# A spectral filter and two gated MLPs on one Trainium2 core: new moments for the hand-made order, with the filter's product and sum behind the subtraction for the lower part of u

## The chip, the cores and the metric

The kernel runs on 1 core of one Trainium2 chip. The metric is device time in microseconds (us), the median of repeated runs. The profile is of one further execution. Engines are named PE (TensorE; PEld is its weight load), DVE (VectorE), ACT (ScalarE), POOL (GpSimd) and SP (SyncE, which issues all DMAs here).

## The reference

Three stages follow each other; B = 8, S = 3072, D = 256.

```
X = rfft(x, axis=1);  y = irfft(X * (filt_r + 1j*filt_i), n=3072)      # per batch
h = y @ w_in;  e = exp(h - max(h));  solu = h * e / sum(e)             # d_ff 1024
ln = (solu - mean) / sqrt(var + 1e-6) * g_ln;  x2 = ln @ w_out
h2 = x2 @ w_in2;  out = (h2 * sigmoid(1.702 * h2)) @ w_out2            # d_ff 2048
```

Everything is float32.

## The kernel before

**Precision.** A product of float32 quality is made of three fp32r matmuls: each operand is split into a high part (an ACT copy to fp32r) and a low part (a subtraction on DVE or POOL), and high*high, low*high and high*low are summed in PSUM.

**Stages.** `Filter` does the FFT filter for one or two batches: 12 steps per batch (`load_x`, `split_x`, `step1`, `store_a`), then 32 groups, each of which goes through nine steps: load (`load2`: gt, bt), `split_m`, `split_a`, `forward`, `swap`, `weigh`, `split_y`, `inverse`, `store_z`. `forward` reads the product f out of PSUM once on ACT (xs, L482) and once on DVE (pr, L485). `swap` exchanges the halves of xs by two DMAs (xw). `weigh` is the product and the sum of the change's name: two DVE instructions, xw = xw*fi (L497) and pr = pr + xw (L498). `split_y` splits pr for the inverse transform.

`First` does the first MLP for a pair of 128-row tiles (a = 0, 1), with 96 pairs in all: `load`, `y`, `y_lo` (xl, L638), `hidden` (L647, four blocks `hidden a f`), `top` (row maximum, L653), `exp` (L659), `weigh` (L672), `square` (L683), `norm` (L692), `shuffle` and `gather` (a trip through DRAM, L699, L705), `turn` (32x32 transposes, L709), `u_hi` (L717), `u_lo` (L720), `project` (L730, four blocks `project c f`), `x2_add`, `x2_hi`, `x2_lo` (L751). A block of `project` needs u of both tiles, so the first one needs `u_lo` of tile 1.

`Second` does the second MLP in 16 steps d per block of two pairs: `hidden` (L799), `tanh` (L806), `gate` (L811), `split_hi` (L817), `split_lo` (gl, L823), `output` (L838); then `finish` and `store`.

**Order.** Every step of every stage gets a moment, a number on a common scale on which a pair takes 16. The steps are then called in the order of their moments, and that is the order of the instructions in each engine's queue; an engine waits at the first instruction that isn't ready. The tables at the top of the file hold the moments: `FIRST` counts from the pair's own zero (two entries: tile 0, tile 1), `SECOND` from the step's own moment, `FILTER` from a slot in the pair ("slots": the groups take the first two), `DENSE` the same for the filter of batches 1 and 2, which has four groups in a pair.

```
r, o, v = 16.0 * (n - 1), First(n), FIRST
at(r + v[step.__name__][a], step, a)
...
for _, _, fn, args in sorted(plan, key=lambda s: s[:2]):
    fn(*args)
```

**Which pairs hold what.** Batch 0 is filtered ahead. While the 12 pairs of batch 0 run, the groups of batches 1 and 2 run (four per pair, 512 columns). Then the filters of batches 3 and 4, and of 5 and 6, each take six pairs of steps with no groups and 16 pairs with two groups (512 columns, "wide" here); the filter of batch 7 takes 16 pairs with two groups of 256 columns ("narrow"). The last 16 pairs have no filter.

Buffers that matter: `ps_h` has one buffer for h, `ps_m` two (yt, f, x2), gt and bt three, mt four, xw, pr, fh and fl two.

Of the kernel before, what the change touches and what calls it, by code (L numbers as in the profile page):

```python
# [36 lines left out]


FIRST = {
    "load": -19.13,  # L40
    "y": -15.7,
    "y_lo": -15.4,
    "hidden": ((-13.6, -11.61), (-3.5, -3.47)),
    "top": (-10.5, -2.4),
    "exp": (-9.6, -1.76),
    "weigh": (-8.86, -1.19),
    "square": (-8.06, 0.3),
    "norm": (-6.58, 0.38),
    "shuffle": (-5.5, 1.2),
    "gather": (-4.79, 1.94),  # L50
    "turn": (-1.56, 6.89),
    "u_hi": (-0.97, 7.3),
    "u_lo": (-0.15, 8.0),
    "project": ((9.4, 10.02), (10.62, 11.52)),
    "x2_add": (10.18, 12.74),
    "x2_hi": 12.79,
    "x2_lo": 13.64,
}

SECOND = {  # L60
    "tanh": 0.7,
    "gate": 1.19,
    "split_hi": 2.47,
    "split_lo": 3.19,
    "output": 4.92,
    "finish": 5.0,
    "store": 6.61,
}


FILTER = {
    "slots": (-0.46, 3.41, 4.53, 14.68),
    "first": (-5.35, -2.02, 0.2, 0.29),
    "second": (-4.91, -1.89, -2.29, -0.1, 1.84, 6.42, 12.49, 15.05, 15.71),
}


DENSE = {
    "start": 15.65,
    "slots": (0.77, 4.65, 8.65, 12.36),  # L80
    "second": (-6.78, -2.67, -1.85, -0.07, 0.61, 5.46, 7.59, 10.89, 10.96),
}

STAGE = [i % 5 if i < 15 else i % 3 for i in range(24)]
# [889 lines left out]
```

## Time and profile before

| | us |
|---|---|
| median of 3 runs | 3728.55 |
| the runs | 3726.52 to 3730.84 |
| span of the profiled execution | 3725.1 |
| PE busy | 3619.2 (97%) |
| DVE busy | 2719.4 (73%) |
| ACT busy | 2054.9 (55%) |
| POOL busy | 809.6 (22%) |

The span runs from the first to the last instruction of one profiled execution, whose own time is this span and what lies around it; the median of the three runs is 3.4 us above the span. A matmul's end is modelled, so the distance from one matmul's start to the next says more than its duration. In the timeline a row holds the start, the time, the engine, the line, the operation, out<-in and a count; a bracket gives the idle time ahead and what ended it.

### The profile page before, as it was taken

The numbers are of one execution on the slowest core, as the hardware profiler recorded it, in microseconds if no ns is written. First come the engines' busy times: TensorE is split into PE (matmuls) and PEld (weight loads), VectorE is DVE, ScalarE is ACT, GpSimd is POOL, SyncE is SP. The second block draws the span as 40 slices with busy tenths as digits, with TensorE's granted clock in tenths as the row PEclk, the third lists the DMA queues.
The fourth block names the chain that finished last, engine by engine and source line by source line (L and its number), as shares of the span: only waits on it lengthen the run. The fifth ranks groups of instructions, "written<-read, shape, count | busy, mean of one in ns | idle before, by whom it ended". The sixth has DMA issues, their size and how long they took to land.

```text
span 3725.1 us, 50469 instructions
## 1 busy us (share of the span) xinstructions
PE 3619.2 (97%) x16768; PEld 2938.3 (79%) x16768; DVE 2719.4 (73%) x4065; ACT 2054.9 (55%) x3762; POOL 809.6 (22%) x1349
## 2 busy tenths in 40 slices
PE   6779999999999999999999999999999999999999
PEld 2367778888888888888888888888888888888887
DVE  7768887667777777667777777667777777766675
ACT  2346665555555555555565656555555555554453
POOL 1123332222222221222222222122122221111110
PEclk7789999999999999999999999999999999999999
DMA  8735554434344433343344433333433332222221
GB/s 256 227 124 149 149 152 125 130 117 117 112 116 115 122 112 108 125 131 108 111 120 117 122 110 117 106 116 104 115 105 102 109 108 77 84 76 77 80 77 32
DMA packets 385669, 433.71 MB, mean 116 GB/s; under 512 B 144128, under 2 KB 294784, under 8 KB 385408
## 3 DMA queue, kind: packets, MB, share of 16 engines
q1 hardware_dynamic: 385408, 430.49, 39.4%
q8 instruction: 132, 2.16, 0.2%
q14 instruction: 129, 1.06, 0.1%
HBM read 232.13 MB, written 176.16 MB: 110 GB/s over the span
## 4 chain that ended last, share of the span: by engine, by line
PE 81%; DVE 8%; DMA 4%; issue 3%; ACT 2%; SPq 1%; POOL 1%; DVEq 0%; POOLq 0%; ACTq 0%
PE h L799 23%; PE o L838 23%; PE x L730 15%; PE h L647 12%; PE f L395 5%; PE yt L629 2%; DVE e L672 1%; DVE u L720 1%; DVE th L811 1%; SPq L861 1%; DMA xin<-in_x 1%; DMA xw<-xs 1%; DVE ob L849 1%; DMA out<-ob 1%; ACT xs L482 1%
## 5 line engine op out<-in xcount | busy, mean ns | idle before, releaser
L838 PE MATMUL o<-gh,w 128*128 128x512 f32 (+1 forms) x3136 | 964.3, 389 | 2.5 <-DVE ob L849 2.5
L799 PE MATMUL h<-x2s,w_hi 128*128 128x512 f32 (+1 forms) x3136 | 958.0, 388 | 2.2 <-DVE x2s L751 2.2
L799 PEld LDWEIGHTS h<-x2s,w_hi 128*128 128x128 f32 x3136 | 572.5, 189 | 118.9 <-DVE x2s L751 2.9
L838 PEld LDWEIGHTS o<-gh,w 128*128 128x128 f32 x3136 | 568.5, 188 | 116.4 <-issue 7.6
L823 DVE TENSOR_TENSOR gl<-th,gh 128x512 fp32r<-128x512 f32 x768 | 541.4, 705 | 153.1 <-ACT gh L817 135.4
L838 PE MATMUL o<-gl,w 128*128 128x512 f32 (+1 forms) x1568 | 607.6, 388 | 0.5 <-DVE gl L823 0.5
L817 ACT CAST gh<-th 128x512 fp32r<-128x512 f32 x768 | 473.2, 616 | 233.1 <-DVE th L811 144.6
L806 ACT ACTIVATE th<-h 128x512 f32<-128x512 f32 x768 | 458.0, 596 | 242.5 <-PE h L799 241.8
L730 PE MATMUL x<-u,w_hi 128*128 128x512 f32 x1536 | 563.7, 404 | 21.2 <-DVE u L720 20.8
L811 DVE SCALAR_TENSOR_TENSOR th<-th,h 128x512 f32<-128x512 f32 x768 | 522.6, 681 | 24.1 <-ACT th L806 21.4
L742 DVE TENSOR_TENSOR x_sum<-x,x_sum 128x256 f32<-128x256 f32 x192 | 81.5, 424 | 563.7 <-ACT x_sum L741 563.6
L799 PE MATMUL h<-x2s,w_lo 128*128 128x512 f32 (+1 forms) x1568 | 479.1, 387 | 0.0
L730 PE MATMUL x<-u,w_lo 128*128 128x256 f32 x1536 | 433.3, 282 | 0.0
L730 PEld LDWEIGHTS x<-u,w_hi 128*128 128x128 f32 x1536 | 291.1, 190 | 112.2 <-DVE u L720 44.8
L659 ACT ACTIVATE e<-h,nmx 128x1024 f32<-128x1024 f32 x192 | 214.6, 1118 | 296.7 <-DVE nmx L653 269.6
L838 PEld LDWEIGHTS o<-gl,w 128*128 128x128 f32 x1568 | 294.7, 188 | 67.8 <-DVE gl L823 6.9
L799 PEld LDWEIGHTS h<-x2s,w_lo 128*128 128x128 f32 x1568 | 293.9, 189 | 62.1
L730 PEld LDWEIGHTS x<-u,w_lo 128*128 128x128 f32 x1536 | 292.9, 191 | 8.9
L663 POOL TENSOR_SCALAR q<-se 128x1 f32<-128x1 f32 x192 | 47.2, 246 | 1129.8 <-ACT e L659 1129.7
L390 POOL TENSOR_TENSOR fl<-bt,fh 96x512 fp32r<-96x512 f32 (+1 forms) x128 | 157.8, 1233 | 589.0 <-ACT fh L389 587.7
L741 ACT COPY x_sum<-x 128x256 f32<-128x256 f32 x192 | 71.0, 370 | 383.2 <-PE x L730 383.2
L653 DVE TENSOR_REDUCE nmx<-h 128x1 f32<-128x1024 f32 x192 | 235.0, 1224 | 19.3 <-PE h L647 5.9
(84 smaller groups left out, 5249.2 us busy)
## 6 DMA issues: line engine op xcount, KB each, us to landing
e_d<-e SPq DMA_DIRECT2D x192, 512.0 KB, 2.9
e<-e_d SPq DMA_DIRECT2D x768, 128.0 KB, 3.0
gt<-in_groups SPq DMA_DIRECT2D x160, 264.0 KB, 3.6
a_d<-az SPq DMA_DIRECT2D x96, 256.0 KB, 2.5
zr<-z_d SPq DMA_DIRECT2D x96, 256.0 KB, 2.8
out<-ob SPq DMA_DIRECT2D x768, 32.0 KB, 1.6
xin<-in_x SPq DMA_DIRECT2D x84, 256.0 KB, 3.0
bt<-a_d SPq DMA_DIRECT2D x96, 192.0 KB, 3.6
```

The source lines that it names most:

```text
L390: engine.tensor_tensor(lo, src, hi, op=ALU.subtract)
L395: nc.tensor.matmul(out, w[i], x[j], start=m == 0, stop=m == 2)
L647: nc.tensor.matmul(hs, xx[:, c, a * P:(a + 1) * P], ww[:, c, f * 512:(f + 1) * 512], start=(m == 0 and c == 0), stop=(m == 2 and c == 1))
L653: nc.vector.tensor_reduce(out=nmx, in_=self.h[a], op=ALU.max, axis=AX.X, negate=True)
L659: nc.scalar.activation(out=e, in_=self.h[a], func=AF.Exp, bias=self.v[a], accum_out=se)
L730: nc.tensor.matmul(self.x2[c][:, :n].rearrange("p i t -> p (i t)"), w2[i][:, kk, c * P:(c + 1) * P], self.u[:, kk, :n].rearrange("p i a t ...
L799: nc.tensor.matmul(self.part(t, j), ww[:, c, f * P:(f + 1) * P], xx[..., c, :], start=(m == 0 and c == 0), stop=(m == 2 and c == 1))
L806: nc.scalar.activation(out=th, in_=self.t[d], func=AF.Tanh, scale=0.851)
L811: nc.vector.scalar_tensor_tensor(out=self.g[d], in0=self.g[d], scalar=1.0, in1=self.t.pop(d), op0=ALU.add, op1=ALU.mult)
L817: nc.scalar.copy(out=gh, in_=self.g[d])
L823: nc.vector.tensor_tensor(gl, th, gh, op=ALU.subtract)
L838: nc.tensor.matmul(o, ww[:, f, h * P:(h + 1) * P], self.part(gg, j), start=(f == 0 and m == 0), stop=(f == K2 - 1 and m == 2))
```

## The change

Only the tables of moments change; each step does what it did. The tables' core:

```diff
 FIRST = {
-    "load": -19.13,
-    "y": -15.7,
-    "y_lo": -15.4,
-    "hidden": ((-13.6, -11.61), (-3.5, -3.47)),
-    "top": (-10.5, -2.4),
-    "exp": (-9.6, -1.76),
-    "weigh": (-8.86, -1.19),
-    "square": (-8.06, 0.3),
-    "norm": (-6.58, 0.38),
-    "shuffle": (-5.5, 1.2),
-    "gather": (-4.79, 1.94),
-    "turn": (-1.56, 6.89),
-    "u_hi": (-0.97, 7.3),
-    "u_lo": (-0.15, 8.0),
-    "project": ((9.4, 10.02), (10.62, 11.52)),
-    "x2_add": (10.18, 12.74),
-    "x2_hi": 12.79,
-    "x2_lo": 13.64,
+    "load": -19.18,
+    "y": -15.41,
+    "y_lo": -14.98,
+    "hidden": ((-13.6, -11.48), (-3.67, -3.45)),
+    "top": (-10.45, -2.27),
+    "exp": (-9.62, -2.21),
+    "weigh": (-8.86, -1.1),
+    "square": (-8.1, 0.3),
+    "norm": (-6.71, 0.45),
+    "shuffle": (-6.64, 1.09),
+    "gather": (-4.79, 2.67),
+    "turn": (-1.22, 6.89),
+    "u_hi": (-1.02, 7.3),
+    "u_lo": (-0.4, 7.44),
+    "project": ((9.08, 10.02), (11.05, 11.52)),
+    "x2_add": (10.24, 12.96),
+    "x2_hi": 13.25,
+    "x2_lo": 13.63,
...
 SECOND = {
     "tanh": 0.7,
     "gate": 1.19,
-    "split_hi": 2.47,
+    "split_hi": 2.49,
     "split_lo": 3.19,
     "output": 4.92,
-    "finish": 5.0,
-    "store": 6.61,
+    "finish": 5.15,
+    "store": 6.9,
...
 FILTER = {
-    "slots": (-0.46, 3.41, 4.53, 14.68),
-    "first": (-5.35, -2.02, 0.2, 0.29),
-    "second": (-4.91, -1.89, -2.29, -0.1, 1.84, 6.42, 12.49, 15.05, 15.71),
+    "slots": (-0.44, 3.27, 3.36, 15.01),
+    "first": (-5.28, -2.04, 0.2, 0.75),
+    "second": (-4.86, -3.09, -2.5, 0.32, 1.88, 9.31, 12.49, 15.49, 15.68),
...
 DENSE = {
     "start": 15.65,
-    "slots": (0.77, 4.65, 8.65, 12.36),
-    "second": (-6.78, -2.67, -1.85, -0.07, 0.61, 5.46, 7.59, 10.89, 10.96),
+    "slots": (0.78, 4.28, 8.58, 12.36),
+    "second": (-6.7, -3.27, -2.21, -0.12, 0.47, 5.53, 7.59, 10.86, 11.01),
```

The nine entries of "second" are the nine steps of a group, in the order given above; the sixth is `weigh`.

## Rows read from the trace of the kernel before

**Rows 1.** The page, part 1: busy time, share of the span, instructions.
```profile
PE 3619.2 (97%) x16768; PEld 2938.3 (79%) x16768; DVE 2719.4 (73%) x4065; ACT 2054.9 (55%) x3762; POOL 809.6 (22%) x1349
```
**Rows 2.** Waits of PE, 880 to 1485 us: total us, times, longest.
```profile
PE x L730 <- DVE u L720: 7.0, 16, 0.5
```
**Rows 3.** Timeline of PE, 1848 to 1892 us (two wide groups in this pair).
```profile
1872.00 0.62 PE L647 MATMUL h<-w_hi,xl 128*128 128x512 f32 x2
...
1884.68 0.39 PE L838 MATMUL o<-gl,w 128*128 128x512 f32 x1
1885.51 0.50 PE L730 MATMUL x<-u,w_hi 128*128 128x512 f32 x1 [0.45 <-DVE u L720]
1885.85 0.28 PE L730 MATMUL x<-u,w_lo 128*128 128x256 f32 x1
```
**Rows 4.** Timeline of PE, 667 to 669.5 us (a pair without groups).
```profile
667.88 0.39 PE L838 MATMUL o<-gl,w 128*128 128x512 f32 x1
668.10 0.39 PE L730 MATMUL x<-u,w_hi 128*128 128x512 f32 x1
668.33 0.28 PE L730 MATMUL x<-u,w_lo 128*128 128x256 f32 x1
```
**Rows 5.** Waits of PE's weight loads, 2545 to 3118 us (narrow groups).
```profile
PEld x L730 <- DVE u L720: 5.9, 16, 0.5
```
**Rows 6.** Timeline of PE, 2798 to 2800 us (narrow groups).
```profile
2798.33 0.39 PE L838 MATMUL o<-gl,w 128*128 128x512 f32 x1
2798.64 0.50 PE L730 MATMUL x<-u,w_hi 128*128 128x512 f32 x1
```
**Rows 7.** Timeline of PE, 435.5 to 438 us (four groups in the pair).
```profile
436.68 0.50 PE L730 MATMUL x<-u,w_hi 128*128 128x512 f32 x1 [0.16 <-DVE u L720]
```
**Rows 8.** Timeline of DVE, 1848 to 1890 us.
```profile
1870.91 0.68 DVE L638 TENSOR_TENSOR xl<-yt,xh 128x512 fp32r<-128x512 f32 x1
...
1878.30 1.23 DVE L653 TENSOR_REDUCE nmx<-h 128x1 f32<-128x1024 f32 x1
1879.44 0.68 DVE L497 TENSOR_TENSOR xw<-xw,gt 96x512 f32<-96x512 f32 x1
1880.15 0.69 DVE L498 TENSOR_TENSOR pr<-xw,pr 96x512 f32<-96x512 f32 x1
1880.76 1.23 DVE L709 STREAM_TRANSPOSE ut<-e 128x1024 f32<-128x1024 f32 x1
1881.92 1.18 DVE L672 SCALAR_TENSOR_TENSOR e<-h,e 128x1024 f32<-128x1024 f32 x1
...
1884.24 1.21 DVE L720 TENSOR_TENSOR u<-ut,u 128x1024 fp32r<-128x1024 f32 x1
```
**Rows 9.** Timeline of ACT, 1848 to 1890 us.
```profile
1858.13 0.60 ACT L806 ACTIVATE th<-h 128x512 f32<-128x512 f32 x1 [2.44 <-PE h L799]
...
1879.56 1.11 ACT L659 ACTIVATE e<-h,nmx 128x1024 f32<-128x1024 f32 x1 [1.99 <-DVE nmx L653]
```
**Rows 10.** Timeline of SP, 1848 to 1890 us: DMA issues.
```profile
1850.55 0.38 SPq L460 DMA_DIRECT2D gt<-in_groups  x1
...
1874.06 1.73 SPq L705 DMA_DIRECT2D e<-e_d  x4
```
**Rows 11.** The tile gt, 1740 to 2360 us: from issue to landing.
```profile
DMA to landing us min/median/max: 3.2/3.6/5.1
```
**Rows 12.** The page, part 6: DMA issues, KB each, median us to landing.
```profile
e<-e_d SPq DMA_DIRECT2D x768, 128.0 KB, 3.0
```
**Rows 13.** Timeline of POOL, 1907 to 1911 us.
```profile
1908.28 1.40 POOL L390 TENSOR_TENSOR fl<-bt,fh 96x512 fp32r<-96x512 f32 x1 [0.59 <-ACT fh L389]
```
**Rows 14.** Timeline of DVE, 1908 to 1911 us.
```profile
1909.05 1.18 DVE L823 TENSOR_TENSOR gl<-th,gh 128x512 fp32r<-128x512 f32 x1
```
**Rows 15.** Timeline of DVE, 165 to 320 us: the first pair's transpose.
```profile
178.92 1.25 DVE L709 STREAM_TRANSPOSE ut<-e 128x1024 f32<-128x1024 f32 x1 [3.74 <-DMA e<-e_d]
```
**Rows 16.** Timeline of PE, 188 to 212 us: first split step of the filter.
```profile
195.30 0.50 PE L395 MATMUL f<-fl,fwd 128*128 128x512 f32 x1 [0.62 <-POOL fl L390]
```

## The prediction

> **What bounds the kernel now.** I read the busy times first. PE is at 97% and DVE at 73% [rows 1], so the time is PE's fixed work plus what PE waits for. Next come PE's waits by stretch. In the stretch with the wide groups of batches 3 and 4 there is one kind of wait: the first block of `project` stands still for DVE's `u_lo`, 16 times in 16 pairs, 7.0 us in all [rows 2]. The stretch of batches 5 and 6 (1770 to 2372 us) repeats that row, so 32 pairs have it. Third, the timeline of PE at that place gives the whole price. In a pair without groups the block starts 0.22 us after the matmul ahead of it, and its second matmul 0.23 us after its first [rows 4]. In a wide pair the same distances are 0.83 and 0.34 us [rows 3]. So the stall costs 0.61 + 0.11 = 0.72 us a pair; the second part, which the table of waits doesn't show, is there whenever the block had to wait at all. With narrow groups the wait shows at the weight load alone, 16 times [rows 5]: 0.31 us against 0.22, and the same long first matmul (0.50 us against 0.39 [rows 4, 6]), so 0.09 + 0.11 = 0.20 us. With four groups in a pair the gap is 0.16 us [rows 7] where a wide pair has 0.45 for its 0.72; I take 0.43 for those.
>
> Why is `u_lo` late? The timeline of DVE shows a row of instructions without a gap between the row maximum `top` at 1878.30 and `u_lo` of tile 1, which ends at 1885.45 [rows 8]. The last matmul ahead of `project` starts at 1884.68, so PE could have begun at 1884.90 [rows 3, 4]. In that row stand the filter's product and sum, at 1879.44 and 1880.15. The transpose `turn` takes their place if they go: 1.32 us.
>
> **The change part by part.** I sorted the moments modulo 16.
>
> **The product and sum.** The group on the first slot had them at -0.46 + 6.42 = 5.96, ahead of `turn` (6.89), `weigh` (7.14), a `split_lo` and a `gate` (7.19) and `u_lo` (8.0). Now they come at -0.44 + 9.31 = 8.87, behind all of these (`u_lo` is now 7.44) and ahead of the `split_lo` of 9.19. So `turn` can start at 1879.44. `weigh` also needs `exp`, which ends at 1879.56 + 1.11 = 1880.67 [rows 9], so it starts some 0.05 us later instead of at 1881.92 [rows 8]: 1.2 us are gained there, not the whole 1.32. `u_lo` then ends near 1884.25, 0.65 us before PE asks for it. The stall goes: 32 x 0.72 = 23.0 us. The narrow groups make the same move: 16 x 0.20 = 3.2 us. In `DENSE` the two stay ahead of `turn` (5.96 against 6.89), so I count nothing there; if that stall went too it would be 8 x 0.43 = 3.4 us more, which is for the range.
>
> What is late next? The two instructions, 1.3 us, now stand ahead of a `split_lo`, a `gate` and `norm`. PE has a block of `project`, a block of the second MLP's `hidden` and another block of `project` to do before it asks for that `split_lo`; `norm` feeds a trip through DRAM whose result is wanted a half pair later. The group on the second slot has its pair of instructions moved too, past `x2_add`, a `split_lo`, a `gate` and the other group's `split_y`, into a place where DVE waits for `project` anyway; `split_y` of that group is still three units later. Cost: nothing. Without that cover it would be their own 1.3 us.
>
> **`x2_lo` ahead of `top` of tile 1, in nearly every pair.** The maximum has to wait for a subtraction of 0.68 us (the nearest row is xl [rows 8]). That could reach `exp`, `square`, `norm` and so xl, for which PE asks next: xl ends at 1871.59 and its matmul starts at 1872.00 [rows 3, 8], 0.41 us to spare. Here the trace shows one more thing. A subtraction on DVE that began while POOL's fl was running (1908.28, 1.40 us [rows 13]) took 1.18 us instead of 0.68 [rows 8, 14]: 0.50 us for the collision. The new place puts `x2_lo` beside POOL's fl of the next group. The delay of xl lies between nothing (the ACT queue also loses a wait of its own there, since `inverse` is moved behind an `output`) and 0.68 + 1.40 = 2.08 us. I take the measured collision: 0.50 - 0.41 = 0.09 us a wide pair, 32 x 0.09 = 2.9 us lost.
>
> The Trainium skill, page "SBUF — State Buffer", section "Who interferes with whom", says that a DVE instruction with two SBUF inputs contends with a GpSimd instruction that reads SBUF, and that the second one blocks fully until the first is done. Rows 13 and 14 agree with it. By that rule alone `x2_lo` would wait for up to the whole 1.40 us, and the sum would be some 16 us worse than mine (0.50 becomes 1.00 if half of fl is left); the slower rival below is this rule carried to its end.
>
> **ACT's new order.** `split_m` now comes ahead of `split_a`, of a `split_hi` and of `square`. Its gt is issued at 1850.55 and lands 3.6, at worst 5.1 us later [rows 10, 11]: 1855.65. The next thing that PE needs of ACT, a `tanh`, can't start before 1858.13, after an idle time of 2.44 us [rows 9]. Cost: nothing; without this cover up to 5.1 - 3.6 = 1.5 us a pair. `split_hi` ahead of `y` delays xh by one copy; the product that reads it stands behind two more blocks of PE.
>
> **PE and SP.** PE swaps neighbours only (an `output` ahead of a `project` block or of `inverse`, `step1` ahead of `hidden`): the same matmuls, and each operand is due earlier than that. On SP `shuffle` of tile 0 goes ahead of some loads of x, stores of a and loads of gt. They then wait for `norm`, but are wanted some three units of the pair's sixteen later. In the start this helps: the first pair's transpose waits 3.74 us for `gather` [rows 15], and its `shuffle` had stood behind those loads. The gain is between 0 and 3.7 us. Against it, `step1` ahead of `hidden` puts that block behind a wait of 0.62 us and a matmul of 0.50 [rows 16], a loss of at most 1.1 us. I take 1.0 us of gain. All other moments change no order, or only one between engines that don't wait for each other.
>
> **The sum**, against the span of 3725.1: -23.0 - 3.2 + 2.9 - 1.0 = -24.3, so 3700.8, and with the 3.4 us by which the median lies above the span 3704.
>
> **The rivals.**
>
> *Half a gain: `turn` now waits for `gather`.* If `turn` goes 1.32 us earlier, the last of its four DMAs must have landed. They are issued from 1874.06 to 1875.79 and take 3.0 us in the median [rows 10, 12]: 1878.8 at the latest issue, 0.65 us ahead of 1879.44. With PE's 0.65 us to spare as well, the landing would have to be 1.3 us late before the stall comes back at all. Half of all pairs also have the sixteen stores of `out` near it. If half of the stalls stay: 3728.55 - 11.5 - 1.6 - 1.0 = 3714.
>
> *No change: the release was not DVE's row.* If `u_lo` is held by ACT's `u_hi` or by `exp` and not by its neighbours, moving these two gives nothing but the start: 3727.5. Against it stands that DVE has no gap between 1878.30 and 1885.45 [rows 8], and that pairs without groups have no wait at all [rows 4].
>
> *Slower: `x2_lo` behind POOL.* The place is DVE's queue just ahead of `top` of tile 1. If the whole 2.08 us reach xl, each wide pair loses 2.08 - 0.41 = 1.67 us and gains 0.72: 32 x 0.95 - 4.2 = +26, so 3755. It turns the gain into a loss from a delay of 0.41 + 27.2/32 = 1.26 us of xl. For it: the collision is real [rows 13, 14]. Against it: the idle time of ACT ahead of `exp` and `inverse`'s wait take up a good part of such a delay.
>
> **How the numbers follow.** My forecast has 0.70, the half gain 0.15, no change 0.09, slower 0.06. The likeliest case's own range is 3698 to 3710: below, the dense stall (3.4) or the start's whole 3.7 us; above, twice the loss that I took and no gain at the start. The range takes in the half gain and, at both ends, the 2 us by which runs differ: 3696 to 3717. A measurement of this kernel can tell about 0.2% (7.5 us) from no change, so faster means below 3721: 0.70 + 0.15 = 0.85; same 0.09; slower 0.06.
>
> **What would show it.** In the changed profile, PE's wait for `u_lo` should be gone from the wide and narrow stretches and still be there with four groups to a pair; L730's first matmul should follow its neighbour by 0.22 us; a wide pair should be some 0.7 us shorter. On DVE, `turn` should follow `top` directly, with L497 and L498 right behind L720. If I am wrong, PE will show a wait at L647 for xl (the slower rival), or DVE one at L709 for `gather` (the half gain); if ACT waits for gt at L470 with PE behind it, my cover there was misread.

## The result, and the profile after

The changed kernel takes 3699.8 us (median of 4 runs, 3699.28 to 3700.02) where the kernel before takes 3728.88 us beside it: a ratio of 0.9919, with a 95% interval of 0.9907 to 0.9932. The forecast was 3704, in a range of 3696 to 3717. Two later groups of runs of the changed kernel gave 3699.65 and 3701.20 us. The profiled execution has a span of 3697.5 us, 27.6 less than before; the granted clock is the same (0.982 of full speed against 0.980).

Part 1 of the page of the changed kernel, to be held against [rows 1]:

```profile
PE 3600.7 (97%) x16768; PEld 2936.2 (79%) x16768; DVE 2772.5 (75%) x4065; ACT 2027.7 (55%) x3762; POOL 869.9 (24%) x1349
```

The instructions are the same, and yet DVE is busy 53 us longer and POOL 60 us. Summed by instruction, `x2_lo` takes 24 us more on DVE, and POOL's L687 (for `norm`) 31 us more: the two engines got in each other's way more, as the last section shows, and the kernel is still faster. That is the first sign that the price of such collisions has to be read at PE.

The whole stretch with the wide groups of batches 3 and 4, by windows, after and then before (length, then busy time and instructions of PE, PEld, DVE, ACT and POOL, PE's clock, the DMAs' share, GB/s):

```profile
864.00:1468.00 604.00, 604.00 (x2833) 497.88 (x2832) 487.51 (x693) 355.82 (x657) 161.65 (x230) 1.00 0.41 116
```
```profile
868.00:1485.00 617.00, 610.02 (x2838) 497.25 (x2837) 476.71 (x691) 362.25 (x655) 152.49 (x229) 1.00 0.40 114
```

Before, PE stood for 7 of 617 us, the wait of [rows 2]. After, it has no wait left there at all. The place of [rows 3] in the changed kernel, timeline of PE:

```profile
1869.18 0.39 PE L838 MATMUL o<-gl,w 128*128 128x512 f32 x1
1869.41 0.39 PE L730 MATMUL x<-u,w_hi 128*128 128x512 f32 x1
1869.64 0.28 PE L730 MATMUL x<-u,w_lo 128*128 128x256 f32 x1
```

0.23 us from each start to the next, as in a pair without groups [rows 4]: both parts of the old price are gone, the gap and the long first matmul. DVE in the same pair, to be held against [rows 8]:

```profile
1862.81 1.23 DVE L653 TENSOR_REDUCE nmx<-h 128x1 f32<-128x1024 f32 x1
1863.95 1.24 DVE L709 STREAM_TRANSPOSE ut<-e 128x1024 f32<-128x1024 f32 x1
1865.31 1.23 DVE L672 SCALAR_TENSOR_TENSOR e<-h,e 128x1024 f32<-128x1024 f32 x1
...
1867.66 1.22 DVE L720 TENSOR_TENSOR u<-ut,u 128x1024 fp32r<-128x1024 f32 x1
1868.80 0.68 DVE L497 TENSOR_TENSOR xw<-xw,gt 96x512 f32<-96x512 f32 x1
1869.51 0.69 DVE L498 TENSOR_TENSOR pr<-xw,pr 96x512 f32<-96x512 f32 x1
```

`turn` follows `top`, and the product and sum follow `u_lo`, which ends at 1868.88, 0.53 us before PE asks for it.

Where the 27.6 us come from shows when each pair is measured from its first matmul of `project` to the next pair's. This table is worked out from the traces, one profiled execution of each kernel, in us; "again" is a second execution of the changed kernel, "+move" is the kernel before with the move of the product and sum alone (the first experiment).

```
stretch                          before    after    again    +move
filter of batch 0, ahead         208.04   208.80   206.66   206.30
pairs 1 to 4                     148.25   144.66   146.33   148.63
pairs 5 to 10 (four groups)      238.99   237.12   238.62   239.15
8 step pairs with finish         292.15   296.46   296.29   292.19
7 step pairs without             257.27   257.23   257.23   257.27
3 pairs at the stages' edges     103.63   103.98   103.97   103.63
32 wide pairs                   1195.34  1171.39  1171.26  1172.15
16 narrow pairs                  568.36   564.74   564.75   564.71
the rest (18 pairs and the end)  713.07   713.10   713.07   712.74
```

The first three stretches differ between executions of the changed kernel by 1.5 to 2.9 us. The others repeat to within 0.2 us, so they resolve what the time of a run (some 2 us of scatter on either side) can't. The wide pairs gave 24.0 us and the narrow ones 3.6. One row goes the other way: the step pairs with a `finish` lost 4.3 us, which no step of the prediction had.

### The profile page after: what moved, and what is told of

It reads as the page before. It is cut to its first block, busy times and chain, and to the rows that moved or that the text cites. A ratio compares the mean times of both kernels' runs of the same rounds, so it can differ in the third digit from the quotient of the medians.

```text
span 3697.5 us, 50701 instructions
## 1 busy us (share of the span) xinstructions
PE 3600.7 (97%) x16768; PEld 2936.2 (79%) x16768; DVE 2772.5 (75%) x4065; ACT 2027.7 (55%) x3762; POOL 869.9 (24%) x1349
## 4 chain that ended last, share of the span: by engine, by line
PE 88%; DVE 2%; ACT 1%; issue 1%; POOL 0%; DMA 0%; POOLq 0%; DVEq 0%; ACTq 0%
PE o L838 27%; PE h L799 27%; PE x L730 14%; PE h L647 13%; PE f L395 5%; PE yt L629 2%; DVE ob L849 0%; DVE gl L823 0%; ACT h L683 0%; DVE xl L638 0%; POOL rs L687 0%; ACT th L806 0%; ACT az L440 0%; ACT u L717 0%; POOL ssq L684 0%
## 5 line engine op out<-in xcount | busy, mean ns | idle before, releaser
L823 DVE TENSOR_TENSOR gl<-th,gh 128x512 fp32r<-128x512 f32 x768 | 557.4, 726 | 132.3 <-ACT gh L817 118.2
L806 ACT ACTIVATE th<-h 128x512 f32<-128x512 f32 x768 | 459.2, 598 | 240.1 <-PE h L799 238.6
L672 DVE SCALAR_TENSOR_TENSOR e<-h,e 128x1024 f32<-128x1024 f32 x192 | 234.2, 1220 | 19.4
L647 PE MATMUL h<-w_hi,xh 128*128 128x512 f32 x768 | 241.4, 396 | 3.1 <-ACT xh L634 3.1
```

Of the source, the lines that this page charges most:

```text
L647: nc.tensor.matmul(hs, xx[:, c, a * P:(a + 1) * P], ww[:, c, f * 512:(f + 1) * 512], start=(m == 0 and c == 0), stop=(m == 2 and c == 1))
L672: nc.vector.scalar_tensor_tensor(out=e, in0=self.h[a], scalar=1.0, in1=e, op0=ALU.mult, op1=ALU.mult, accum_out=su)
L806: nc.scalar.activation(out=th, in_=self.t[d], func=AF.Tanh, scale=0.851)
L823: nc.vector.tensor_tensor(gl, th, gh, op=ALU.subtract)
```

## The experiments

All times are medians beside runs of the kernel before on the same chip; ratios are to those.

### The move of the product and sum alone

The kernel before, with one number changed:

```diff
 FILTER = {
-    "second": (-4.91, -1.89, -2.29, -0.1, 1.84, 6.42, 12.49, 15.05, 15.71),
+    "second": (-4.91, -1.89, -2.29, -0.1, 1.84, 9.31, 12.49, 15.05, 15.71),
```

> The kernel before with one number changed: the moment of the filter's product and sum in wide and narrow groups, 6.42 to 9.31. Theory (these two, standing in DVE's row between the maximum and the transpose, held the subtraction for u's lower part late): the 32 stalls of 0.72 us and the 16 of 0.20 us go, so 23.0 + 3.2 = 26.2 us less than before, 3701 to 3704. Rival (the gain rests on the rest of the reordering as well, for example on the gather that is late next): half of it or less, 3715 or more.

Measured: 3698.58 us, ratio 0.9925 (0.9912 to 0.9937). That is 2.4 us under the expected range. By stage the wide pairs give 23.2 us and the narrow ones 3.65, and nothing else moves beyond its scatter; the filter ahead of batch 0, which scatters most, is 1.7 us shorter in this execution. The theory holds and its price too (23.0 and 3.2 were forecast). This one number is worth as much as the whole change: what the other new moments give and take by stage adds up to nothing that the time shows.

### The changed kernel without that move

```diff
 FILTER = {
-    "second": (-4.86, -3.09, -2.5, 0.32, 1.88, 9.31, 12.49, 15.49, 15.68),
+    "second": (-4.86, -3.09, -2.5, 0.32, 1.88, 6.42, 12.49, 15.49, 15.68),
```

> The changed kernel with only that moment set back, 9.31 to 6.42. Theory (the move is what paid): the wide and narrow pairs get their stalls back, 24 + 3.7 us by the traces of the two kernels, so 3724 to 3728. Rival (the other new moments alone also bring the subtraction forward): under 3712.

Measured: 3725.29 us, ratio 0.9995 (0.9986 to 1.0004): no gain is left, and the theory holds. PE's waits from 880 to 1485 us show the row of [rows 2] again:

```profile
PE x L730 <- DVE u L720: 6.9, 16, 0.5
```

### Product and sum behind the transpose, but still ahead of `u_lo`

The kernel before with 7.9 in place of 6.42. It tells whether the two did harm because of what they preceded (`turn`, `weigh`) or only because they stood ahead of `u_lo`.

```diff
 FILTER = {
-    "second": (-4.91, -1.89, -2.29, -0.1, 1.84, 6.42, 12.49, 15.05, 15.71),
+    "second": (-4.91, -1.89, -2.29, -0.1, 1.84, 7.9, 12.49, 15.05, 15.71),
```

> The kernel before with the product and sum at 7.9 in place of 6.42: behind the transpose and the weighting of tile 0, still ahead of the subtraction for u's lower part. Theory (DVE works through a row without a gap, so only the work ahead of that subtraction counts, not its order): the stall stays, within 3 us of the kernel before, 3725 to 3731. Rival (the product and sum did harm by holding up the transpose or the weighting): part of the gain, 3700 to 3717.

Measured: 3737.75 us, ratio 1.0024 (1.0014 to 1.0033), slower than forecast by either. The rival falls at once: nothing is gained. DVE of this kernel in a wide pair:

```profile
1923.80 1.23 DVE L709 STREAM_TRANSPOSE ut<-e 128x1024 f32<-128x1024 f32 x1
1925.15 1.23 DVE L672 SCALAR_TENSOR_TENSOR e<-h,e 128x1024 f32<-128x1024 f32 x1
...
1927.50 0.68 DVE L497 TENSOR_TENSOR xw<-xw,gt 96x512 f32<-96x512 f32 x1
1928.22 0.69 DVE L498 TENSOR_TENSOR pr<-xw,pr 96x512 f32<-96x512 f32 x1
1928.83 1.21 DVE L720 TENSOR_TENSOR u<-ut,u 128x1024 fp32r<-128x1024 f32 x1
```

and PE's wait for it:

```profile
1930.09 0.50 PE L730 MATMUL x<-u,w_hi 128*128 128x512 f32 x1 [0.68 <-DVE u L720]
```

The gap of [rows 3] has grown from 0.45 to 0.68 us, and the 32 wide pairs by 7.7 us, 0.24 each (the narrow ones by 3.1). My expectation took DVE's row as work alone. But `weigh` needs ACT's `exp`, which ends at 1925.03 here, just as the transpose does: with the product and sum ahead, DVE had other work while `exp` finished; with them behind it stands still until 1925.15, 0.12 us. From the start of `turn` to that of `weigh` it is now 1.35 us instead of 1.16 [rows 8], and `weigh` takes 1.23 instead of 1.18 us. The first alone makes 0.19 of the 0.24. The same 0.12 stands in the changed kernel, ahead of its `weigh` at 1865.31, where the 1.32 us that went away cover it.

### The slot of the step pairs

In the step pairs the changed kernel has one new wait of PE, in the table of its waits over the whole span:

```profile
PE o L838 <- DVE gl L823: 2.3, 8, 0.3
```

Eight times, once for each step pair with a `finish`. The place in one of them, PE, then DVE, then POOL of the changed kernel:

```profile
688.30 0.61 PE L838 MATMUL o<-gh,w 128*128 128x512 f32 x2
689.21 0.50 PE L838 MATMUL o<-gl,w 128*128 128x512 f32 x1 [0.29 <-DVE gl L823]
```
```profile
686.37 1.44 DVE L849 STREAM_TRANSPOSE ob<-o 128x256 f32<-128x256 f32 x4
687.73 1.43 DVE L823 TENSOR_TENSOR gl<-th,gh 128x512 fp32r<-128x512 f32 x1
```
```profile
686.07 2.54 POOL L390 TENSOR_TENSOR fl<-xin,fh 128x512 fp32r<-128x512 f32 x2 [1.06 <-ACT fh L389]
```

POOL now runs two subtractions of `split_x` back to back, until 688.61. DVE's gl comes behind the four transposes of `finish`, so it can't start earlier, and takes 1.43 us where its mean is 0.73. The third entry of "slots" (4.53 to 3.36) put the two steps together. So it was set back in the changed kernel:

```diff
 FILTER = {
-    "slots": (-0.44, 3.27, 3.36, 15.01),
+    "slots": (-0.44, 3.27, 4.53, 15.01),
```

> The changed kernel with the third number of the filter's slots set back, 3.36 to 4.53, so that the two split_x of a step pair no longer follow each other directly. Theory (two of POOL's subtractions of split_x back to back cover DVE's gl behind finish, which takes 1.43 us in place of 0.85, and PE waits 0.56 us for it): the loss goes in 8 pairs, 8 x 0.56 = 4.5 us, so about 3695.4. Rival (the loss comes from finish and split_hi, whose moments were moved too): no difference, 3699 to 3700.

Measured: 3696.85 us, ratio 0.9919 (0.9905 to 0.9932). The eight pairs take 292.25 us in place of 296.46, all of the loss. The time alone didn't settle it, since the changed kernel hadn't run beside it. So the two were run in one group.

> The changed kernel with the third slot back at 4.53, a second time, now with the changed kernel itself beside it on the same chip. Theory: the eight step pairs take 292.2 us in place of 296.4, and the time is 4.3 us under that of the changed kernel beside it. Rival (the time of the step pairs is given back later): the same time.

> The changed kernel, beside the two others of this group on one chip. Expected by every theory: 3698 to 3700.

Measured: 3695.44 us (3694.47 to 3696.83), ratio 0.9909 (0.9896 to 0.9923), against 3701.20 (3699.96 to 3702.73, a little above the expected 3698 to 3700) for the changed kernel beside it. The spans of the two profiled executions are 4.9 us apart: 4.0 of it lie in the eight pairs (292.25 against 296.28) and 1.6 in the first three stretches, within their scatter; the step pairs without a `finish` and the narrow pairs are 0.3 us longer each. The theory holds, and this kernel has the lowest median of the study. The same place in its first run, PE, DVE, POOL:

```profile
690.38 0.62 PE L838 MATMUL o<-gh,w 128*128 128x512 f32 x2
690.83 0.39 PE L838 MATMUL o<-gl,w 128*128 128x512 f32 x1
```
```profile
689.79 0.65 DVE L823 TENSOR_TENSOR gl<-th,gh 128x512 fp32r<-128x512 f32 x1
```
```profile
688.13 1.29 POOL L390 TENSOR_TENSOR fl<-xin,fh 128x512 fp32r<-128x512 f32 x1 [1.06 <-ACT fh L389]
692.34 1.30 POOL L390 TENSOR_TENSOR fl<-xin,fh 128x512 fp32r<-128x512 f32 x1 [2.92 <-ACT fh L389]
```

`finish` is where it was in the changed kernel; POOL's second subtraction is 2.9 us later, gl takes 0.65 us, and PE's distance is back from 0.91 to 0.45 us.

### `x2_lo` behind the maximum again

```diff
 FIRST = {
-    "x2_lo": 13.63,
+    "x2_lo": 13.74,
```

> The changed kernel with the moment of x2_lo set from 13.63 to 13.74, which puts it behind the maximum of tile 1 again, as before the change. Theory (its collision with POOL's fl is taken up ahead of xl, so the place costs nothing): within 2 us of the changed kernel. Rival (it does cost the 2.9 us of the prediction, 32 x 0.09): 3 us faster. Second rival (x2_lo ahead of the maximum helps, since the second MLP gets its operand earlier): 2 us or more slower.

In the same group of runs stood the changed kernel itself.

> The changed kernel once more, beside the kernels of this group on one chip, so that their times are compared with its own time there. Expected by every theory: 3698 to 3700.

Measured: 3703.22 us (3696.31 to 3707.72), ratio 0.9932 (0.9919 to 0.9944), against 3699.65 (3696.61 to 3701.23) and 0.9923. The intervals overlap, so I go by stage: the wide pairs take 1171.1 us, against 1171.3 to 1171.4 in three executions of the changed kernel. The place costs these pairs 0.2 to 0.3 us in all, not 2.9: the first rival falls. The old place costs 1.3 to 1.4 us more in the step pairs with a `finish` (297.73) and 0.5 to 0.6 in the narrow ones, 2 us in all, where the second rival begins. But its reason isn't seen: PE waits for `x2_lo` of this kernel only twice, 2.3 us in the first four pairs, which are not longer for it (145.05). So the theory holds for the wide pairs; for the whole kernel the new place is the better one by some 2 us, for a reason that was not traced.

Still the collision is there, in every wide pair. The group of `x2_lo`'s instructions, 864 to 1468 us, of the changed kernel and then of this one (busy us, mean ns):

```profile
L751 DVE TENSOR_TENSOR x2s<-x_sum,x2s 128x512 fp32r<-128x512 f32 x16 | 18.4, 1152 | 0.0
```
```profile
L751 DVE TENSOR_TENSOR x2s<-x_sum,x2s 128x512 fp32r<-128x512 f32 x16 | 10.9, 683 | 0.0
```

It takes 0.47 us more, close to the 0.50 taken from [rows 13, 14]. What becomes of that on the way to xl, in us after the pair's first matmul of `project` (from the traces: the pair that begins at 1885.51 in [rows 3], its counterpart in the changed kernel, and the one with `x2_lo` back behind the maximum):

```
                                 before    after    x2_lo back
DVE top starts                    12.82    13.58    12.73
ACT exp starts                    14.09    14.83    13.99
ACT square starts                 19.42    19.69    19.34
POOL L684 (for norm) starts       20.76    21.05    20.69
POOL L684 takes                    0.77     0.27     0.27
POOL L687 ends                    22.18    21.97    21.61
DVE xl ends                       23.63    23.42    23.06
PE's first matmul with xl         24.03    23.91    23.91
```

The last two columns differ by the place of `x2_lo` alone. It makes `top` start 0.85 us later and `square` only 0.35: ACT takes up most of the difference, since without the move it stands still for 0.38 us between `exp` and `square`, waiting for the product of an `inverse`. The 0.36 us that reach xl come out of PE's spare time, which is 0.85 us without the move and 0.49 with it. That there is so much to spare is owed to the other new moments: before, POOL's L684 took 0.77 us beside an fl of DVE, and it takes 0.27 in both kernels in which DVE's fl comes earlier. So xl is ready 0.21 us earlier than before, although `x2_lo` holds it up.

### The slot of the pairs with four groups

The stall of [rows 7] went too, although there the product and sum stay where they were. In the trace, `forward` of the second group now runs ahead of a `hidden` of the second MLP on PE, and pr (L485), ahead of which DVE waited before, starts 0.7 to 0.95 us earlier in these pairs than before. To test this, the second slot goes back behind that `hidden`:

```diff
 DENSE = {
-    "slots": (0.78, 4.28, 8.58, 12.36),
+    "slots": (0.78, 4.5, 8.58, 12.36),
```

> The changed kernel with the second slot of the pairs with four groups set from 4.28 to 4.5, which puts that group's forward behind hidden of the second MLP on PE again. Theory (forward ahead of hidden let DVE's product start 0.95 us earlier and so took the stall of project away in those pairs): the stall of 0.43 us is back in 5 pairs, about 2.2 us, so about 3702. Rival (the other new moments of these pairs, such as split_a ahead of exp on ACT, took it away): 3699 to 3700.

Measured: 3702.68 us, ratio 0.9935 (0.9923 to 0.9948). Pairs 5 to 10 take 239.65 us, against 237.1 to 238.6 in three executions of the changed kernel, and the stall is back in each of them. First PE, and DVE in the pair after it, of the changed kernel, then the same of this one:

```profile
433.03 0.39 PE L838 MATMUL o<-gl,w 128*128 128x512 f32 x1
433.26 0.39 PE L730 MATMUL x<-u,w_hi 128*128 128x512 f32 x1
```
```profile
463.15 0.69 DVE L390 TENSOR_TENSOR fl<-pr,fh 96x512 fp32r<-96x512 f32 x1
463.93 0.69 DVE L485 TENSOR_TENSOR pr<-f,gt 96x512 f32<-96x512 f32 x1
```
```profile
435.43 0.39 PE L838 MATMUL o<-gl,w 128*128 128x512 f32 x1
436.03 0.50 PE L730 MATMUL x<-u,w_hi 128*128 128x512 f32 x1 [0.22 <-DVE u L720]
```
```profile
466.03 0.69 DVE L390 TENSOR_TENSOR fl<-pr,fh 96x512 fp32r<-96x512 f32 x1
467.70 0.69 DVE L485 TENSOR_TENSOR pr<-f,gt 96x512 f32<-96x512 f32 x1 [0.98 <-ACT xs L482]
```

With `forward` in its old place DVE waits 0.98 us for ACT's copy of f ahead of pr, and everything behind it, `u_lo` too, is that much later. The theory holds.

### The start

`shuffle` of tile 0 back behind the loads:

```diff
 FIRST = {
-    "shuffle": (-6.64, 1.09),
+    "shuffle": (-5.5, 1.09),
```

> The changed kernel with shuffle of tile 0 set from -6.64 back to -5.5, behind the loads and stores on SP. Theory (its earlier issue is what made the first four pairs of batch 0 some 3 us shorter): those pairs go back from 144.7 to about 148, and the time rises by 2 to 3 us. Rival (the gain of these pairs came from other new moments, such as step1 ahead of hidden on PE): they stay at 144 to 146, and the time stays.

Measured: 3702.34 us, ratio 0.9933 (0.9921 to 0.9945). That is 2.7 us above the changed kernel beside it, as the theory had it, but of the 1.3 us between the two profiled executions only 0.9 lie in pairs 1 to 4. These take 147.26 us: between the 144.66 to 146.33 of three executions of the changed kernel and the 148.25 to 148.68 of three with the old `FIRST`. So I also gave the kernel before this part, with the move and the dense slot:

```diff
 FIRST = {
-    "norm": (-6.58, 0.38),
-    "shuffle": (-5.5, 1.2),
+    "norm": (-6.71, 0.38),
+    "shuffle": (-6.64, 1.2),
...
 FILTER = {
-    "second": (-4.91, -1.89, -2.29, -0.1, 1.84, 6.42, 12.49, 15.05, 15.71),
+    "second": (-4.91, -1.89, -2.29, -0.1, 1.84, 9.31, 12.49, 15.05, 15.71),
...
 DENSE = {
-    "slots": (0.77, 4.65, 8.65, 12.36),
+    "slots": (0.77, 4.28, 8.65, 12.36),
```

> The kernel before with three of the change's parts alone: product and sum at 9.31; the second slot of the pairs with four groups at 4.28; shuffle of tile 0 at -6.64 (with norm at -6.71, so that it still comes first). Theory (these three hold all that the change gained, and the loss in the step pairs belongs to the slot that is left as it was): by stage against before, wide and narrow pairs -27 together, dense pairs -1 to -2, pairs 1 to 4 -2 to -3, step pairs 0; in all 30 to 32 us, 3696 to 3698. Rival for the start (step1 ahead of hidden brought those 2 to 3 us, not shuffle): pairs 1 to 4 stay at 148.

Measured: 3698.83 us, ratio 0.9918 (0.9905 to 0.9932). That is 29.6 us under the kernel before, where 30 to 32 were expected. By stage: wide and narrow 26.9 us less than before, pairs 5 to 10 2.1 less, the step pairs 292.16, all as expected. Pairs 1 to 4 take 148.85: an early `shuffle` alone gives nothing. So the theory that it alone made the gain of the start falls. Taking it back cost 0.9 to 1.6 us in one execution, where these pairs scatter by 1.7; whether it has a share beside other moments, and which other moment brings the 2.8 us of these pairs (145.7 in the mean of three executions, against 148.5), stays open. That it is `step1` was not tried by itself.

## Why the prediction was right, and where its steps were off

| term of the sum | forecast | measured, by stage |
|---|---|---|
| wide pairs: the stall, and `x2_lo` against POOL | -23.0 + 2.9 | -24.0 together; the move alone -23.2, the place of `x2_lo` +0.2 to +0.3 |
| narrow pairs | -3.2 | -3.6; the move alone -3.65 |
| start (pairs 1 to 4) | -1.0 | -3.6 here; -2.8 in the mean of three |
| pairs 5 to 10 | 0 | -1.9 here; -0.4 to -1.9 in three |
| step pairs with `finish` | 0 | +4.3 |
| the rest | 0 | +1.1 |
| sum, against the span | -24.3 | -27.6 |

**The core was right, in mechanism and in size.** The stall was the work ahead of `u_lo` in DVE's row, it cost 0.72 us, and it went whole. The part that the table of waits doesn't show (the long first matmul after a wait) had to be in the price: PE's waits alone [rows 2] would give 14 us, and 23.2 were measured. The margin is 0.53 us where 0.65 was forecast: `weigh` starts 0.12 us after `exp` ends, not 0.05, and takes 0.05 us longer.

**Too dear: the collision of `x2_lo`.** The step that failed is "0.50 - 0.41 = 0.09 us a wide pair". The 0.50 was right (0.47). What was wrong is that a delay ahead of `top` would reach xl whole, with only 0.41 us in its way. I counted the spare time at the last instruction alone, and that of the kernel before. Of 0.85 us at `top`, ACT's idle time took up all but some 0.36, and the other new moments had raised the spare time of xl to 0.85 us. The "some 16 us worse" doesn't follow either: with half of fl left, 0.70 us, an end 0.55 us after POOL's (as in [rows 13, 14]) makes an instruction of 1.25 us, 0.57 more than 0.68 and not 1.00.

**Not seen: the step pairs.** The step that failed is "All other moments change no order, or only one between engines that don't wait for each other". The slot 4.53 to 3.36 moves a whole `split_x`, and POOL and DVE do wait for each other, with no semaphore between them. [Rows 13, 14] had shown the effect and I used it in one place only. That was the dearest error, +4.3 us.

**Not seen: the pairs with four groups.** The same step of the prediction. "In `DENSE` the two stay ahead of `turn` (5.96 against 6.89), so I count nothing there" held for the two instructions; it was `forward` on PE that freed DVE's row. The gain lies within the bound of 3.4 us that the range had.

**The start** was within its bound (0 to 3.7 us), but the reason given, `shuffle`, doesn't carry it.

These errors cancel in part: the wide pairs came out 3.9 us lower than forecast, the start 2.6, the pairs with four groups 1.9 and the narrow ones 0.4, and the step pairs 4.3 higher, the rest 1.1. These add up to 14 us, and the sum is off by 3.3: that 3704 came within 4.2 us of 3699.8 is in part luck. The median stands 2.3 us above the span here, not 3.4; each run lies 1.8 us above its own span, so the rest is scatter of the profiled executions. The 0.8 us of the wide pairs beyond the move alone were not traced.

**The rivals.** *Half a gain*: `turn` does wait for `gather` now and then, in the wide stretch of batches 3 and 4 three times in 33:

```profile
DVE ut L709 <- DMA e<-e_d: 1.0, 3, 0.5
```

At most 0.5 us, which the margin took up; no wait of PE came of it. *No change* falls with the first experiment. Of the arguments against it, "pairs without groups have no wait at all" holds for the step pairs only: among the last 16 pairs PE's weight load waits for `u_lo` in 8 (2.6 us in all), and the change leaves that as it is (7 times, 2.3 us). *Slower*: PE has no wait for xl in the wide pairs. **The cover for gt**: ACT does wait for it now, 864 to 1468 us,

```profile
ACT mt L470 <- DMA gt<-in_groups: 16.5, 15, 2.9
```

and PE stands for none of it; that cover held, with up to 2.9 us used where I had counted 1.5.

## What to carry to other kernels

An in-order queue is a sum: what stands ahead of a late instruction counts, and to move work within that part of the queue gained nothing here; it even uncovered a wait that the work had hidden. A move of 1.3 us of work past the late instruction gave all the gain here, by one number of more than fifty. For every step moved, put the other engine's instructions that now run beside it next to it too, since two engines can hold each other up without a semaphore, and take the spare time along the whole chain, not at its last link. Where the time of a run scatters by 2 us, stretches of the trace cut at the same instruction of each pair told apart effects of a few hundredths of a us a pair.

## What the runs showed of the hardware that was not expected

**A blocked subtraction of DVE ended 0.55 us after POOL's.** Three places: gl of [rows 14] ends at 1910.23, the fl of [rows 13] at 1909.68; gl of the step pair ends at 689.16, POOL at 688.61; and `x2_lo` of the changed kernel, DVE and then POOL:

```profile
1845.18 1.18 DVE L751 TENSOR_TENSOR x2s<-x_sum,x2s 128x512 fp32r<-128x512 f32 x1
```
```profile
1844.20 1.61 POOL L390 TENSOR_TENSOR fl<-bt,fh 96x512 fp32r<-96x512 f32 x1 [3.23 <-ACT fh L389]
```

ends at 1846.36 and 1845.81. In the whole trace of the changed kernel 47 of the `x2_lo` began while POOL's fl ran, and all ended 0.55 us after it; DVE's products of 256 columns (L497) that began while POOL's L471 ran ended 0.28 us after it. The collision is thus no fixed toll of 0.50 us, as I had used it: DVE's instruction stands until POOL's is done and then does most of its work. What it costs is what is left of POOL's instruction when DVE's comes up, and with two of POOL's in a row it stood through the rest of the second. The Trainium skill, page "SBUF — State Buffer", section "Summary: rules for kernel authors", says just that (the second one to issue blocks fully until the first finishes), and the three places agree. The rule didn't make this change slower because ACT's idle time and the spare time of xl took up the delay.

**It goes both ways.** The product and sum in their new place, with the gl behind them, cover POOL's two instructions that feed `norm`:

```profile
1868.57 0.96 POOL L684 TENSOR_SCALAR ssq<-ssq,q 128x1 f32<-128x1 f32 x1 [1.38 <-ACT h L683]
1869.62 1.62 POOL L687 TENSOR_TENSOR rs<-ssq,half 128x1 f32<-128x1 f32 x1
```

Elsewhere in the same stretch these take 0.27 and 0.57 us. In these traces such a block shows as a longer instruction and not as a wait with a releaser, so the table of waits doesn't hold it.
